# Retention followed by a Mish feed-forward layer: the decay of later chunks' keys goes into k, and v is loaded as bf16

## The chip, the core and the metric

The kernel runs on one core of one Trainium2 chip. The metric is device time in microseconds (us) of one execution. The core has a matrix engine (PE; its weight loads are listed apart as PEld), a vector engine (DVE), a scalar engine (ACT), GpSimd (POOL), a sync engine (SP), and 16 DMA engines that all queues share. In this kernel POOL issues nearly all loads, SP issues stores and DMA transposes.

## The reference

Eight batches, eight heads, 576 positions, 64 values per head. Retention is attention without a softmax: scores are multiplied by a power of a per-head decay. Its output goes through a two-layer feed-forward block (512 to 2048 to 512) with Mish between.

```python
def _attn_ref(q, k, v):
    scale = 1.0 / np.sqrt(D_)
    scores = scale * np.matmul(q, k.transpose(0, 1, 3, 2))
    gamma = 1.0 - 2.0 ** (-5.0 - np.arange(H))
    rel = pos[:, None] - pos[None, :]
    Dmat = np.where(rel >= 0, gamma[:, None, None] ** rel[None], 0.0)
    return np.matmul(scores * Dmat, v)
...
def _moe_ref(x, w_in, w_out):
    h = x @ w_in
    g = h * np.tanh(log1p(exp(h)))
    return g @ w_out
```

The decay from key position j to query position i is gamma to the power i - j, so it splits into a factor on q (gamma to the i, with 1/8 folded in) and a factor gamma to the minus j, which may stand on k or on v.

## The kernel before, in words

The 4608 rows are cut into 36 chunks of 128 rows. Chunks 0 to 7 are the first 128 positions of each batch; chunks 8 to 35 (`N0` = 8 and on) are the later ones, where a chunk may hold the last 64 positions of two batches. Four chunks form one of nine tiles `t`. The schedule is written out by hand: what stands first in the program is issued first on each engine.

The first eight chunks have their own path (`f_transpose`, `f_scores`, `f_out`), which applies the decay as a full matrix `dmask` and takes v unscaled; `f_state` scales a copy of their v with `gv` (L257) for the running state.

The later chunks go through these steps:

- `load(n)` or `load_part(n, part)` issues the transfers of q, k and v from POOL's queue (L325, and L329 for the chunks of two half batches). q and k land in `qkraw`, v in `vraw`, all as f32. For chunks 10 to 17 `load` first copies one element of an earlier v (L313), so that POOL waits until that v has landed. Later loads are paced by `tick` (L1045), a one-element copy of a result of the running tile, for which POOL waits.
- `step_p(n)`, "P", multiplies q and k with `gqk` on DVE and writes bf16 into `qks` (L341, two instructions per chunk). The column for k is all ones.
- `step_v(n)`, "V", multiplies v with `gv` and writes bf16 into `vs` (L348): on DVE for chunks 8 to 15, on POOL for chunks 16 to 35.
- `step_t(n)` transposes `qks` into `qkT`: on PE with a copy by ACT for chunks below 16, and by a DMA transpose from SP (L370) for the others.
- `states(n)` makes products of k in `qks` and `vs` (L428), which DVE adds into running states (L452, L450); `step_s` makes the scores (L382), `step_m` masks them (L388); `outputs` multiplies masked scores with `vs` (L484) and `outputs_end` adds the part of the earlier state (L500). `visit`, or `visit_first` and `visit_second`, run these for two chunks at a time, once in about 14 us.

Beside them PE works through the feed-forward layer: `g1` (L570, L575) with Mish on ACT (L586), and the second product from seven half-size products per tile (`seven`, L662), whose sums of operands DVE makes (L653, and L643 for the weights) and whose results DVE, ACT and POOL add up. In the last tile the first product is also made from seven products (`last`, L778). Their sums go through `both` and `z` (L790 to L808), for which `vraw` buffers are used, and `one`, in a `vs` buffer.

Of the kernel before, what the change touches and what calls it, by code (L numbers as in the profile page):

```python
# [9 lines left out]
F32 = mybir.dt.float32  # L10
BF16 = mybir.dt.bfloat16
AX = mybir.ActivationFunctionType
OP = mybir.AluOpType
# [3 lines left out]
def kernel(  # L17
# [21 lines left out]
    P = 128  # L39
# [4 lines left out]
    KC = d_model // P  # L44
    NCH = 4
    NPE = 16
    NV = 16
    PF = 5


# [102 lines left out]
    nc.vector.tensor_scalar(ident, dist, 0.0, None, op0=OP.is_equal)  # L153

    gqk = consts.tile([P, 5, 2, H], F32)
    nc.vector.memset(gqk, 1.0)
    gq = gqk[:, :, 0, :]
    gv = consts.tile([P, 5, H], F32)
    warm = consts.tile([P, 1], F32)

    def keep_warm(n, pool=ps_o, name="ops"):
# [146 lines left out]
    def load(n):  # L308
        if n >= n_chunks:
            return  # L310
        if N0 + 2 <= n < NPE + 2:

            nc.gpsimd.tensor_copy(landed[:, n % 2:n % 2 + 1], live[n - 2]["v"][:, H - 1, D - 1:D])  # L313
        for part in range(3):
            load_part(n, part)

    def load_part(n, part):
        b, c = chunks[n]
        if n not in live:
            qkr = io.tile([P, 2, H, D], F32, name="qkraw")  # L320
            live[n] = {"qkr": qkr, "v": io.tile([P, H, D], F32, name="vraw", bufs=7)}
        qkr, vr = live[n]["qkr"], live[n]["v"]
        for t, src in (((qkr[:, 0], q), (qkr[:, 1], k), (vr, v))[part],):
            if c < 4:
                nc.gpsimd.dma_start(  # L325
                    out=t, in_=src[b, :, ds(P * c, P), :].rearrange("h p d -> p h d"))
            else:
                for e in range(2):
                    nc.gpsimd.dma_start(  # L329
                        out=t[ds(64 * e, 64)],  # L330
                        in_=src[b + e, :, ds(512, 64), :].rearrange("h p d -> p h d"))

    def step_p(n):
        c = chunks[n][1]
        qks = io.tile([P, 2, H, D], BF16, name="qks", bufs=4)
        live[n]["qks"] = qks
        slots = qks.rearrange("p i (g x y) d -> p (i g) y x d", x=2, y=2)
        heads = live[n]["qkr"].rearrange("p i (g y x) d -> p (i g) y x d", x=2, y=2)
        factors = gqk[:, c].rearrange("p i (g y x) -> p (i g) y x", x=2, y=2)
        for y in range(2):  # L340
            nc.vector.tensor_tensor(slots[:, :, y], heads[:, :, y],  # L341
                                    factors[:, :, y].unsqueeze(3).to_broadcast([P, NP, 2, D]), op=OP.mult)

    def step_v(n):
        c = chunks[n][1]
        vs = tok.tile([P, H, D], BF16, name="vs")
        engine = nc.vector if n < NV else nc.gpsimd
        engine.tensor_tensor(vs, live[n]["v"], gv[:, c, :].unsqueeze(2).to_broadcast([P, H, D]), op=OP.mult)  # L348
        live[n]["vs"] = vs

    def step_t(n):
        flat = live[n]["qks"].rearrange("p i h d -> p (i h d)")
# [416 lines left out]
    def last(t):  # L769

        gts[t] = gp.tile([P, nF, NCH * P], BF16, name="gT")
        flat = gts[t].rearrange("p f i -> p (f i)")
        tt = nc.vector.tensor_tensor
        crossed = []

        def small(to, i, b, start=False):
            for c in range(hK):
                nc.tensor.matmul(to, lhsT=w7[i][:, c, b, :], rhs=x7[i][:, c, :], start=(start and c == 0),  # L778
                                 stop=(c == hK - 1), skip_group_check=True)

        def pair(b, between, adds=0):

            across = ps_h.tile([P, 2, hT], F32, name="hp")
            along = ps_sc.tile([P, 2, hT], F32, name="sc")
            small(across[:, 0], 3, b, True)
            small(across[:, 1], 4, b)
            small(along[:, 1], 6, b, True)
            small(along[:, 0], 1, b)
            both = io.tile([P, H, D], F32, name="vraw", bufs=7).rearrange("p h d -> p (h d)")
            act(both, across.rearrange("p a i -> p (a i)"))  # L790
            one = tok.tile([P, H, D], BF16, name="vs").rearrange("p h d -> p (h d)").bitcast(F32)
            act(one, along[:, 0])
            run(crossed)
            z = io.tile([P, H, D], F32, name="vraw", bufs=7).rearrange("p h d -> p (h d)")
            z = z.rearrange("p (a i) -> p a i", a=2)
            nc.gpsimd.tensor_tensor(z[:, 0], both[:, 0:hT], both[:, hT:2 * hT], op=OP.add)  # L796
            nc.gpsimd.tensor_tensor(z[:, 1], z[:, 0], one, op=OP.add)
            for _ in range(adds):
                behind_visit.pop(0)()
            between()  # L800
            small(across[:, 0], 5, b)
            small(across[:, 1], 2, b)
            small(along[:, 0], 7, b)
            o = 2 * b * NCH * P
            tt(z, z, across, op=OP.subtract)
            tt(z, along, z, op=OP.add)
            to = flat[:, ds(o, 6 * hT)].rearrange("p (a i) -> p a i", a=2)[:, :, 0:hT]
            crossed.append(lambda: nc.scalar.activation(to, z, AX.Mish))  # L808
            crossed.append(lambda: nc.scalar.activation(flat[:, ds(o + hT, 2 * hT)],
                                                        across.rearrange("p a i -> p (a i)"), AX.Mish))  # L810

        sums_at = {0: 1, 2: 6, 3: 5, 4: 7}
        g_sum(t - 1, 2)
        for b in range(nB - 1):
            pair(b, lambda: unit(t - 1, 2 * b), {3: 2, 4: 1}.get(b, 0))
            if b in sums_at:
                g_sum(t - 1, sums_at[b])
            unit(t - 1, 2 * b + 1)
        pair(nB - 1, lambda: unit(t - 1, 12), 1)
        unit(t - 1, 13)  # L820
        run(crossed)
        g1(t, nF - 2)
        g1(t, nF - 1, (ps_st, "st"))
# [61 lines left out]
    def att(n, steps):  # L885
        if n >= n_chunks:
            return
        for step in steps:
            {"P": step_p, "V": step_v, "T": step_t}[step](n)

    nc.scalar.activation(dmask, dmask, AX.Exp, bias=lnd[:, 0:1])
    for h in range(H):
# [84 lines left out]


    ps = {0: 0, 4: 1, 8: 2, 11: 3}
    vs = {0: 0, 5: 1, 9: 2, 13: 3, 18: 4, 19: 5}  # L980
    ts_ = {4: 0, 7: 1, 12: 2, 14: 3, 19: 4, 21: 5}
    FIRST = {1: (0, 0), 2: (1, 0), 3: ("turn", 1), 5: (0, 1), 6: (1, 1)}
    for u in range(24):
        j, w = divmod(u, 4)
        halved[0] = 2 if u < 1 else 0
        if u in FIRST:
            what, of = FIRST[u]
            if what == "turn":
                f_k0_copy(of, f_k0(of), (dve, act))
            else:  # L990
                first_states(of, what)
                if what:
                    first_states_copy(of, act)
        if u in ps:
            att(N0 + ps[u], "P")
        if u == 11:
            step_m(N0)
        if u in vs:
            att(N0 + vs[u], "V")
        if u in (1, 2):  # L1000
            f_state(1, u + 1, nc.vector)
        for what in {7: "W4", 9: "W6 W3 W1", 19: "S1", 21: "S6"}.get(u, "").split():
            w_sum(int(what[1])) if what[0] == "W" else g_sum(1, int(what[1]))
        if w == 0 and j > 0:
            if j < 5:
                load(N0 + j + 3)
            else:
                more_loads(N0 + j + PF)
        if u == 10:
            units = states(N0)  # L1010
            units[0]()
            step_s(N0)
            units[1]()
            run(sums)
        elif u == 16:
            att(N0 + 4, "P")
            visit(N0, ((ps_o, "ops"), (ps_h, "hp")), (act, act), masked=False)
            g_sum(1, 2)
            run(sums)
            att(N0 + 5, "P")  # L1020
            step_m(N0 + 2)
        elif u == 22:
            visit(N0 + 2, ((ps_h, "hp"), (ps_h, "hp")), (act, act))
        if u in (13, 20):
            run(casts, dve if u == 13 else act)
        if u in ts_:
            att(N0 + ts_[u], "T")
        if u < nF:
            g1(1, u)
            flush()  # L1030
        else:
            unit(1, u - nF)
# [9 lines left out]
    def tick(t, i):  # L1042

        f = done.get(t, 0)
        nc.gpsimd.tensor_copy(held[:, i % 2:i % 2 + 1], gts[t][:, f, 0:1])  # L1045

    W_IN = {3: 1, 4: 2, 8: 6, 10: 5, 11: 7}
    for t in range(NS, nT - 1):
        for i in range(nF):
# [39 lines left out]
                rest()  # L1089
            if w == 0 and n + 2 == NPE:  # L1090
                tick(t, i)
            if w in ((4,) if n + 2 < NPE else (0, 1)) and n <= NPE - 2:
                for m in (0, 1) if w == 4 else (w,):
                    att(n + 2 + m, "V")
            if n + 2 >= NPE and w == (6 if n + 2 == NPE else 3) and n + 4 < n_chunks:
                tick(t, i)
                att(n + 4, "V")
                att(n + 5, "V")
            if w == 7 and n + 4 == NPE:
                att(n + 5, "T")  # L1100
            if w == (4 if n <= NPE - 2 else 7) and n + 4 >= NPE:
# [67 lines left out]
```

## Time and profile before

| what | value |
|---|---|
| time, median of 3 runs | 290.36 us (288.36 to 295.45) |
| the profiled execution | 288.53 us, with a span of 286.8 us |
| busy: PE, DVE, ACT, POOL | 276.7, 215.5, 162.1, 172.0 us |
| granted PE clock | 1.00 throughout |
| transfers from POOL (q0) | 14256 packets, 30.15 MB |
| transfers from SP (q1) | 26656 packets, 14.69 MB |
| v loads | 24 of 256 KB, 8 of 128 KB; median 5.4 and 5.3 us to landing |

The span is the time from the first to the last instruction that the profiler recorded; the execution's own time holds 1.7 us more around it. Busy times are sums over instructions of an engine. Bytes are counted as they land, so a transfer that casts f32 to bf16 counts half of what it reads.

### The profile page before, as it was taken

What the parts mean: (1) busy time and instruction counts of PE and PEld (TensorE: products, weight loads), DVE (VectorE), ACT (ScalarE), POOL (GpSimd) and SP (SyncE); (2) the same over time, 40 slices, a digit from 0 to 9 for tenths busy, and PEclk for the clock granted to TensorE, in tenths of its full rate; (3) what the DMA queues carried; (4) which work ended last, traced back from release to release, by engine and by line L of the source; (5) the groups of instructions that cost most, each with busy time, mean ns of one, the idle gap of its engine ahead of it and who ended that gap; (6) DMA issues with size and microseconds to landing.
All of it is one profiled execution on the core that took longest, in us unless ns stands there. A gap on an engine that the chain in (4) does not pass through costs nothing.

```text
span 286.8 us, 8923 instructions
## 1 busy us (share of the span) xinstructions
PE 276.7 (96%) x3818; PEld 192.9 (67%) x3854; DVE 215.5 (75%) x302; ACT 162.1 (57%) x286; POOL 172.0 (60%) x243
## 2 busy tenths in 40 slices
PE   7799999999999999999999999999999999999994
PEld 3466775556876667666766666667666766888783
DVE  4740459999999996896599757974899194777783
ACT  5566415777776564565465555564566556476620
POOL 8686861687793999697929682969240000469500
PEclk9999999999999999999999999999999999999999
DMA  7999999978799994979599999697968001200323
GB/s 150 205 204 205 204 238 220 305 186 210 190 215 197 166 279 122 210 189 233 145 153 209 141 209 204 167 206 189 154 101 146 2 3 73 75 1 3 108 92 94
DMA packets 41545, 45.94 MB, mean 160 GB/s; under 512 B 23841, under 2 KB 31265, under 8 KB 41505
## 3 DMA queue, kind: packets, MB, share of 16 engines
q0 software_dynamic: 14256, 30.15, 50.1%
q1 hardware_dynamic: 26656, 14.69, 26.4%
q8 instruction: 30, 0.49, 0.8%
q10 hardware_dynamic: 592, 0.52, 0.6%
q14 instruction: 11, 0.08, 0.1%
HBM read 36.70 MB, written 9.44 MB: 161 GB/s over the span
## 4 chain that ended last, share of the span: by engine, by line
PE 69%; DMA 15%; DVE 7%; POOL 5%; issue 2%; ACT 1%; POOLq 0%; ACTq 0%; DVEq 0%
PE hp L570 28%; PE ops L662 27%; DMA w_out_t<-in_moe_w_out_dram 4%; DMA vraw<-in_v_dram 4%; DMA w_in_t<-in_moe_w_in_dram 4%; PE st L662 2%; DMA qkraw<-in_k_dram 2%; PE hp L662 2%; PE hp L778 2%; DVE qks L341 2%; PE sc L778 1%; PE sc L428 1%; PE sc L382 1%; PE sc L849 1%; POOL gT L107 1%
## 5 line engine op out<-in xcount | busy, mean ns | idle before, releaser
L570 PE MATMUL hp<-xT,w_in_t 128*128 128x512 bf16 x439 | 111.8, 379 | 1.8 <-issue 0.3
L586 ACT ACTIVATE gT<-hp 128x512 bf16<-128x512 f32 x129 | 76.9, 600 | 46.6 <-PE hp L570 42.2
L570 PEld LDWEIGHTS <-w_in_t 128*128 128x128 bf16 x474 | 45.3, 98 | 41.0 <-issue 0.9
L662 PEld LDWEIGHTS <-room 128*128 128x128 bf16 x608 | 58.8, 98 | 13.9 <-DVE room L653 0.3
L341 DVE TENSOR_TENSOR qks<-qkraw,gqk 128x512 bf16<-128x512 f32 x56 | 48.1, 908 | 10.1 <-issue 5.1
L653 DVE TENSOR_TENSOR room<-gT 128x2048 bf16<-128x2048 bf16 x40 | 50.8, 1289 | 1.1 <-ACT gT L586 1.1
L1045 POOL COPY held<-gT 128x1 bf16<-128x1 bf16 x58 | 23.0, 397 | 32.9 <-ACT gT L586 32.9
L662 PE MATMUL ops<-room,room 128*128 128x256 bf16 x320 | 40.1, 273 | 0.3 <-DVE room L653 0.2
L796 POOL TENSOR_TENSOR vraw<-vraw 128x256 f32<-128x256 f32 x7 | 6.5, 924 | 37.9 <-ACT vraw L790 37.8
L662 PEld LDWEIGHTS <-gT 128*128 128x128 bf16 x256 | 24.5, 98 | 6.2 <-ACT gT L586 0.4
L388 DVE TENSOR_TENSOR sm<-sc,mask 128x1024 bf16<-128x1024 f32 x14 | 17.1, 1218 | 11.7 <-PE sc L382 11.1
L348 POOL TENSOR_TENSOR vs<-vraw,gv 128x512 bf16<-128x512 f32 x20 | 25.5, 1297 | 0.0
L662 PE MATMUL ops<-w_out_t,room 128*128 128x256 bf16 x208 | 25.3, 273 | 0.0
L325 POOL DMA_DIRECT2D vraw<-in_v_dram x24 | 21.3, 886 | 2.5 <-DMA w_out_t<-in_moe_w_out_dram 1.4
L325 POOL DMA_DIRECT2D qkraw<-in_q_dram x24 | 21.7, 904 | 1.5 <-issue 1.2
L325 POOL DMA_DIRECT2D qkraw<-in_k_dram x24 | 21.2, 884 | 0.0
L452 DVE TENSOR_TENSOR total<-sc,total 128x256 f32<-128x256 f32 x32 | 13.5, 422 | 2.2 <-PE sc L428 1.4
L512 ACT CAST xT<-hp 128x512 bf16<-128x512 f32 x19 | 10.3, 589 | 7.6 <-PE hp L500 7.6
L662 PE MATMUL ops<-room,gT 128*128 128x256 bf16 x112 | 13.7, 272 | 0.2 <-ACT gT L586 0.2
L575 PE MATMUL hp<-xT,w_in_t 128*128 128x256 bf16 x92 | 13.8, 273 | 0.0
L575 PEld LDWEIGHTS <-w_in_t 128*128 128x128 bf16 x92 | 9.0, 98 | 5.4
L175 DVE COPY room<-gT 128x1024 bf16<-128x1024 bf16 x4 | 3.2, 828 | 9.7 <-DMA gT<-in_q_dram 9.7
(186 smaller groups left out, 423.6 us busy)
## 6 DMA issues: line engine op xcount, KB each, us to landing
out_dram<-res SPq DMA_DIRECT2D x29, 256.0 KB, 4.8
qkraw<-in_q_dram POOLq DMA_DIRECT2D x24, 256.0 KB, 6.1
qkraw<-in_k_dram POOLq DMA_DIRECT2D x24, 256.0 KB, 6.4
vraw<-in_v_dram POOLq DMA_DIRECT2D x24, 256.0 KB, 5.4
w_out_t<-in_moe_w_out_dram POOLq DMA_DIRECT2D x4, 512.0 KB, 11.3
w_in_t<-in_moe_w_in_dram POOLq DMA_DIRECT2D x3, 512.0 KB, 10.1
out_dram<-res SPq DMA_DIRECT2D x9, 128.0 KB, 2.4
gT<-in_k_dram POOLq DMA_DIRECT2D x8, 128.0 KB, 6.9
```

Source lines behind the costliest of these rows:

```text
L325: nc.gpsimd.dma_start(out=t, in_=src[b, :, ds(P * c, P), :].rearrange("h p d -> p h d"))
L341: nc.vector.tensor_tensor(slots[:, :, y], heads[:, :, y], factors[:, :, y].unsqueeze(3).to_broadcast([P, NP, 2, D]), op=OP.mult)
L348: engine.tensor_tensor(vs, live[n]["v"], gv[:, c, :].unsqueeze(2).to_broadcast([P, H, D]), op=OP.mult)
L388: nc.vector.tensor_tensor(sm.rearrange("p e x n i -> p (e x n) i"), live[n]["sc"].rearrange("p e x n i -> p (e x n) i"), mask.unsqueeze(1) ...
L452: nc.vector.tensor_tensor(new[:, k], st[:, j, x], total[b], op=OP.add)
L512: copy(xts[t][:, :, ds(P * s, 2 * P)].rearrange("p h (x j i) -> p j h x i", x=2, j=2)[:, j], both[j])
L570: nc.tensor.matmul(to, lhsT=w, rhs=x, start=first, stop=last)
L575: nc.tensor.matmul(to[:, ts(j, n)], lhsT=w, rhs=x[:, ts(j, n)], start=False, stop=False, skip_group_check=True)
L586: nc.scalar.activation(gts[t][:, f, :], hp, AX.Mish)
L653: engine.tensor_tensor(to, g_half(t, *a), g_half(t, *b), op=op_)
L662: nc.tensor.matmul(bank[:, half, :], lhsT=g[:, f, ts(half, P)], rhs=w[:, f, :], start=(f == 0 and half == 0 and not add), stop=(f == hF - ...
L1045: nc.gpsimd.tensor_copy(held[:, i % 2:i % 2 + 1], gts[t][:, f, 0:1])
```

## The change

The factor gamma to the minus j moves from v to k for the later chunks. The k column of `gqk`, ones before, becomes `gv`, so the multiplication that `step_p` already does brings it in. `step_v` disappears with its calls, on DVE and on POOL, as do the ticks directly ahead of those of its calls that ran on POOL (not the ticks ahead of loads). v is loaded straight into `vs` in bf16: source f32, destination bf16, a casting transfer at the same place in POOL's queue. `vs` has 13 buffers where it had 6, `qks` 6 where it had 4, and the 7 f32 buffers of `vraw` are gone; `both` and `z` of the last tile use `qks` buffers. The first eight chunks keep their scaled copy of v.

```diff
     gqk = consts.tile([P, 5, 2, H], F32)
-    nc.vector.memset(gqk, 1.0)
     gq = gqk[:, :, 0, :]
-    gv = consts.tile([P, 5, H], F32)
+    gv = gqk[:, :, 1, :]
...
-            nc.gpsimd.tensor_copy(landed[:, n % 2:n % 2 + 1], live[n - 2]["v"][:, H - 1, D - 1:D])
+            nc.gpsimd.tensor_copy(landed[:, n % 2:n % 2 + 1], live[n - 2]["vs"][:, H - 1, D - 1:D])
...
-            live[n] = {"qkr": qkr, "v": io.tile([P, H, D], F32, name="vraw", bufs=7)}
-        qkr, vr = live[n]["qkr"], live[n]["v"]
+            live[n] = {"qkr": qkr, "vs": tok.tile([P, H, D], BF16, name="vs", bufs=13)}
+        qkr, vr = live[n]["qkr"], live[n]["vs"]
...
-        qks = io.tile([P, 2, H, D], BF16, name="qks", bufs=4)
+        qks = io.tile([P, 2, H, D], BF16, name="qks", bufs=6)
...
-    def step_v(n):
-        c = chunks[n][1]
-        vs = tok.tile([P, H, D], BF16, name="vs")
-        engine = nc.vector if n < NV else nc.gpsimd
-        engine.tensor_tensor(vs, live[n]["v"], gv[:, c, :].unsqueeze(2).to_broadcast([P, H, D]), op=OP.mult)
-        live[n]["vs"] = vs
...
-            both = io.tile([P, H, D], F32, name="vraw", bufs=7).rearrange("p h d -> p (h d)")
+            both = io.tile([P, 2, H, D], BF16, name="qks", bufs=6).rearrange("p i h d -> p (i h d)").bitcast(F32)
...
-            z = io.tile([P, H, D], F32, name="vraw", bufs=7).rearrange("p h d -> p (h d)")
+            z = io.tile([P, 2, H, D], BF16, name="qks", bufs=6).rearrange("p i h d -> p (i h d)").bitcast(F32)
...
-        if u in vs:
-            att(N0 + vs[u], "V")
...
-            if w in ((4,) if n + 2 < NPE else (0, 1)) and n <= NPE - 2:
-                for m in (0, 1) if w == 4 else (w,):
-                    att(n + 2 + m, "V")
-            if n + 2 >= NPE and w == (6 if n + 2 == NPE else 3) and n + 4 < n_chunks:
-                tick(t, i)
-                att(n + 4, "V")
-                att(n + 5, "V")
```

More of the change, by code (lines that the diff above doesn't have):

```diff
@@ L46 @@
     NPE = 16
-    NV = 16
     PF = 5
@@ L788, in pair @@
             small(along[:, 0], 1, b)
-            both = io.tile([P, H, D], F32, name="vraw", bufs=7).rearrange("p h d -> p (h d)")
+            both = io.tile([P, 2, H, D], BF16, name="qks", bufs=6).rearrange("p i h d -> p (i h d)").bitcast(F32)
             act(both, across.rearrange("p a i -> p (a i)"))
-            one = tok.tile([P, H, D], BF16, name="vs").rearrange("p h d -> p (h d)").bitcast(F32)
+            one = tok.tile([P, H, D], BF16, name="vs", bufs=13).rearrange("p h d -> p (h d)").bitcast(F32)
             act(one, along[:, 0])
             run(crossed)
-            z = io.tile([P, H, D], F32, name="vraw", bufs=7).rearrange("p h d -> p (h d)")
+            z = io.tile([P, 2, H, D], BF16, name="qks", bufs=6).rearrange("p i h d -> p (i h d)").bitcast(F32)
             z = z.rearrange("p (a i) -> p a i", a=2)
@@ L888, in att @@
         for step in steps:
-            {"P": step_p, "V": step_v, "T": step_t}[step](n)
+            {"P": step_p, "T": step_t}[step](n)
     nc.scalar.activation(dmask, dmask, AX.Exp, bias=lnd[:, 0:1])
@@ L979 @@
     ps = {0: 0, 4: 1, 8: 2, 11: 3}
-    vs = {0: 0, 5: 1, 9: 2, 13: 3, 18: 4, 19: 5}
     ts_ = {4: 0, 7: 1, 12: 2, 14: 3, 19: 4, 21: 5}
```

## The prediction

> **What bounds the kernel now.** I read the page's busy row first, then busy time by stage, then who waited for whom on PE, and last single stretches of the PE timeline.
>
> ```profile
> span 286.8 us, 8923 instructions
> PE 276.7 (96%) x3818; PEld 192.9 (67%) x3854; DVE 215.5 (75%) x302; ACT 162.1 (57%) x286; POOL 172.0 (60%) x243
> ```
>
> PE is busy for 276.7 of 286.8 us, so 10.1 us at most can be won without taking matmuls away, and the change takes none away. The view by stages (length, then busy us of PE, PEld, DVE, ACT and POOL, the granted clock, the DMA share, GB/s) says where those 10.1 us lie:
>
> ```profile
> 0.00:20.00 20.00, 16.27 (x186) 9.34 (x189) 11.75 (x39) 11.43 (x21) 15.49 (x29) 1.00 1.02 185
> 20.00:264.00 244.00, 241.74 (x3476) 168.13 (x3508) 188.12 (x243) 143.38 (x253) 151.58 (x211) 1.00 0.81 164
> 264.00:286.80 22.80, 18.65 (x161) 15.42 (x159) 15.67 (x21) 7.29 (x14) 4.97 (x5) 1.00 0.31 93
> ```
>
> The start has 3.73 us of idle PE and the end 4.15 us. In the 244 us between, where every operation of this change lies except a memset and the sums of the last tile, PE idles for 2.26 us. A busy PE can still be a slow one, so I compared spacings (start, length, engine and line, operation, tiles, count):
>
> ```profile
> 71.17 1.04 PE L662 MATMUL st<-w_out_t,gT 128*128 128x256 bf16 x8
> 72.04 0.61 PE L362 MATMUL hp<-ident,qks 128*128 128x128 bf16 x8
> ...
> 277.48 1.91 PE L662 MATMUL ops<-room,room 128*128 128x256 bf16 x16
> 279.22 1.91 PE L662 MATMUL hp<-room,room 128*128 128x256 bf16 x16
> ```
>
> At 71 us, in the stretch where DVE is 99% busy, 8 matmuls take 72.04 - 71.17 = 0.87 us, 109 ns each. In the tail, with all operands ready, 16 take 279.22 - 277.48 = 1.74 us, 109 ns each. So PE runs at its own pace already. Its waits say the same (total us, times, longest); these are among the largest after the first 12 us:
>
> ```profile
> PE sc L212 <- DVE room L216: 0.4, 2, 0.3
> PE ops L662 <- DVE room L653: 0.2, 1, 0.2
> PE ops L662 <- ACT gT L586: 0.2, 1, 0.2
> ```
>
> The Trainium skill (Perfetto Trace Analysis, "Identifying the Most-Contended Engine") warns of this reading: matmul busy time flatters PE, and weight-load busy time is the better measure. By its 67% a third of the span would be open; the equal spacing of 109 ns does not agree, and I follow the spacing. What would follow if PE had room is the third rival.
>
> The chain of waits none the less runs through DMA and DVE until 77 us, and there lies what the change touches (start, length, what):
>
> ```profile
> 36.91 12.21 DMA vraw<-in_v_dram
> ...
> 50.61 6.68 DMA qkraw<-in_k_dram
> 57.39 1.29 DVE qks L341 x2
> ...
> 74.81 1.20 DVE vs L348 x2
> 76.00 1.15 DVE room L653
> 77.20 1.92 PE ops L662 x16
> ```
>
> This chain had no slack at 77.20, but PE waited only 0.23 us there (the 0.2 in the view of waits): it had other work until then.
>
> **The change, part by part.**
>
> ```profile
> L341 DVE TENSOR_TENSOR qks<-qkraw,gqk 128x512 bf16<-128x512 f32 x56 | 48.1, 908 | 10.1 <-issue 5.1 <-DMA qkraw<-in_q_dram 2.6 <-DMA qkraw<-in_k_dram 2.5
> L348 POOL TENSOR_TENSOR vs<-vraw,gv 128x512 bf16<-128x512 f32 x20 | 25.5, 1297 | 0.0
> L348 DVE TENSOR_TENSOR vs<-vraw,gv 128x512 bf16<-128x512 f32 x8 | 5.3, 684 | 0.0
> ```
>
> *Scaling of v, removed.* DVE loses 8 instructions, 5.3 us, between 51.2 and 85.9 us. Four of them lie on the chain behind 57.39 (0.60 + 0.60 + 1.20 = 2.4 us), so L653 can end 2.4 us sooner. PE gets of that its wait, 0.23 us; the rest is early data for a busy engine. POOL loses 20 instructions, 25.5 us, and 9 of its 58 one-element copies at L1045 (397 ns each, 3.6 us). L341's median is 685 ns and its mean 908, and its long ones (2.13 us for two, at 92.4) coincide with L348 on POOL (2.95 us from 92.5); without it, DVE regains up to 48.1 - 56 x 0.685 = 9.7 us. After 86 us none of this is on PE's path: 0 us. The cover is PE's queue of ready matmuls. If it were gone, DVE's 5.3 + 9.7 us would count.
>
> *Decay in k.* step_p multiplies the same tile with another factor column: same instruction, 0 us. The memset at L156 (0.12 us on DVE at 4.61) goes; DVE waits 0.61 us for PE at 7.07 behind it, so 0 us. The exponential that made gv now writes into gqk, 40 values either way.
>
> *v by casting transfers.* Each issue stays on POOL's queue at its old place: 24 of 882 ns and 8 of 691 ns. Nearest rows for a casting issue: the two 256-column w_in loads and three of 512 columns average 769 ns (L86), w_out 836 ns (L89), with 4 runs per partition against 8 for v; I take no change, and up to 0.2 us more each would still leave POOL 25.5 + 3.6 - 32 x 0.2 = 22.7 us lighter.
>
> What the transfer itself costs is not in the trace; nothing there writes v's 64 values as 128 bytes. Rows (the last three values are clock, DMA share and GB/s, counted as landed):
>
> ```profile
> 24.00:28.00 4.00, 3.95 (x29) 2.79 (x29) 0.00 (x0) 2.89 (x5) 2.13 (x4) 1.00 1.24 206
> 46.00:48.00 2.00, 2.00 (x37) 1.33 (x37) 2.00 (x3) 1.52 (x3) 0.00 (x0) 1.00 1.05 219
> 92.00:96.00 4.00, 4.00 (x24) 2.19 (x23) 4.00 (x6) 2.81 (x6) 4.00 (x5) 1.00 1.26 134
> ```
>
> At 46 us plain loads of q, k and v drain in 256-byte runs at 219 GB/s: 262 KB take 1.20 us. At 24 us casting loads with long runs land 206 GB/s: v's 131 KB would take 0.64 us. At 92 us, with transposes in flight, 134 GB/s is nearly the worst rate at a full share: 0.98 us. If a run costs what it costs now, whatever its length, it stays 1.20 us. So -0.56 to 0 us a transfer by the rows; I take 0, because v keeps its 1024 runs. The worse case, above every row, is the second rival.
>
> *Waits and buffers.* PE's state products (L428) and output products (L484) now wait for the transfer of v itself instead of L348. Queued behind such a wait would be all of PE. For chunk 10 the transfer has landed by 58.64 us (POOL's copy L313 that waits for it starts then) and the product starts at 68.16: 9.5 us of cover. A load now overwrites what PE reads, with 13 buffers: the first reuse, chunk 21 at 97.15 us, needs chunk 8's products, done by 69.3. Sums of the last tile move from vraw's buffers into the 6 of qks, reused three pairs later; the last transposes out of them are issued at 215-217 us and land in 10.6 us at most, before L790 at 245.9. All 0 us. SP's queue is unchanged.
>
> **Sum.** -0.23 us (L653's wait), with the issue gaps beside it -0.3. Span 286.8 - 0.3 = 286.5; the profiled execution has 288.53 - 286.8 = 1.73 around it: 288.2. The median of the runs shown is 290.36, 1.83 above the profiled execution, so 290.0.
>
> **The rivals.**
> 1. *All of PE's small gaps close.* Lighter DVE and POOL take away the whole 2.26 us between 20 and 264: 290.36 - 2.26 = 288.1. For: several gaps stand behind DVE or ACT. Against: most are single gaps of 0.05 us named "issue". Chance 0.12.
> 2. *The casting transfers are slow, and k comes late.* Between 40 and 58 us the DMA share is 1.01 to 1.06, so extra transfer time delays what is queued behind it. Two v transfers (chunks 8 and 9) are ahead of k of chunk 10, which ends the wait at 57.30. The chain behind has 2.4 us of removed DVE work as cover and 0.23 us of wait already. At twice 1.20 us the delay is 2.4 and just covered; from there it decides. At three times it is 4.8 - 2.4 = 2.4 us of stall: 290.36 + 2.4 = 292.8; at four times 295.2; a 2% loss takes more than that, with later loads late too. Against: no row is over 1.20 us. Chance 0.13. The Trainium skill (DMA: Bandwidth & Descriptors, "Specifications") speaks for it: under 512 bytes a transfer turns into read-modify-write, and v's runs go from 256 to 128. The trace shows plain 256-byte runs at 219 GB/s landed where long casting runs read twice 206, which agrees that short runs are slow, but cannot tell 128 from 256.
> 3. *PE has room, and DVE is the bound where it is full.* From 57 to 100 us DVE is 99% busy. It would give back its 5.3 us of L348 and, at 92 to 96 us, 1.1 us of lengthened L341: 290.36 - 6.4 = 284.0. Against: the spacing at 71 us. Chance 0.05.
>
> That the change does not do what it says I exclude: no L348 is left on any queue, and every other engine's order stands.
>
> **How the numbers follow.** The forecast has 0.70. Range: rival 1 less 1.1 us for runs that stand apart (the two lower ones differ by 2.0) gives 287.0; rival 2 at three times with 0.7 on top gives 293.5. About 2% (5.8 us) is what a measurement of this kernel can tell from no change. Faster by more: rival 3, 0.05. Slower by more: half of rival 2, since waits on later loads could add up, 0.07. Within: 0.88.
>
> **What would show it.** Right: PE busy again near 276.7 with no wait over 0.3 us after 20 us, DVE near 215.5 - 15 = 200, POOL near 143, L341's mean near 685 ns, the step at 77.20 no longer behind DVE. Wrong: PE waits on in_v_dram or on qks at 57 to 80 us, or v's time to landing well above 5.4 us.

## The result, and the profile after

The changed kernel takes 287.56 us in the median (287.32 to 287.91, 7 runs), the kernel before 288.92 us on the same chip (288.36 to 295.45, 7 runs). The ratio is 0.9941, with a 95% interval of 0.9914 to 0.9967: 0.6% faster, below the 2% that count as a difference here, but clear of 1. Ratios leave disturbed executions out; the medians hold them. The profiled executions agree: 288.53 us before, 287.56 after, with spans of 286.8 and 285.9.

The page after, its busy row, the queue of POOL's transfers, and the groups that the change touches (lines are shifted: L341 is now L339, L1045 is L1033, L653 is L644, L662 is L653):

```profile
span 285.9 us, 8908 instructions
PE 276.9 (97%) x3818; PEld 192.7 (67%) x3854; DVE 197.3 (69%) x293; ACT 162.1 (57%) x286; POOL 144.2 (50%) x214
...
q0 software_dynamic: 41136, 26.48, 56.1%
...
L339 DVE TENSOR_TENSOR qks<-qkraw,gqk 128x512 bf16<-128x512 f32 x56 | 35.4, 685 | 4.5 <-issue 2.9
...
vs<-in_v_dram POOLq DMA_DIRECT2D x24, 128.0 KB, 5.1
```

PE is as busy as before (276.9 against 276.7 us). DVE lost 18.2 us and POOL 27.8 us, and a span that is 0.9 us shorter is all that is left of these 46 us. The multiplication of q and k, which had a mean of 908 ns, now has its median of 685 ns as its mean. The transfers carry fewer bytes (26.48 against 30.15 MB) in nearly three times the packets (41136 against 14256) and their packet times add up to a larger share of the engines' span (56.1 against 50.1%).

By stages (length, then busy us of PE, PEld, DVE, ACT and POOL, clock, DMA share, GB/s):

```profile
0.00:20.00 20.00, 17.38 (x189) 9.70 (x192) 11.92 (x38) 11.71 (x21) 16.13 (x30) 1.00 1.01 192
20.00:264.00 244.00, 242.17 (x3484) 168.74 (x3516) 171.03 (x236) 143.83 (x254) 124.31 (x182) 1.00 0.86 149
264.00:285.90 21.90, 17.35 (x148) 14.23 (x147) 14.37 (x20) 6.52 (x12) 3.75 (x4) 1.00 0.31 97
```

In the first 20 us PE's busy time leaves 2.62 us where it left 3.73, in the long middle stage 1.83 where it left 2.26. Most of the latter is not idling. Both pages count 3818 matmuls and 3854 weight loads, so 36 matmul records are missing. In two later runs, `e_plain` and `e_memset`, the page counts 3854 of each. In both, PE is busy for the whole of the middle stage; this is the first:

```profile
20.00:264.00 244.00, 244.00 (x3517) 168.68 (x3516) 170.84 (x236) 143.62 (x254) 123.28 (x182) 1.00 0.71 164
```

With 33 more matmuls recorded than after (3517 against 3484), nothing is left of the 1.83 us. So the prediction's 2.26 us were some 0.4 us of pauses, and what went is the 0.43 us between the two figures. In the timeline before, PE has two marked pauses in this stage; after, none:

```profile
77.20 1.92 PE L662 MATMUL ops<-room,room 128*128 128x256 bf16 x16 [0.23 <-DVE room L653]
...
171.72 0.59 PE L570 MATMUL hp<-xT,w_in_t 128*128 128x512 bf16 x2 [0.26 <-issue]
```

The step that the prediction built on, in the timeline of DVE, before and then after:

```profile
75.92 2.35 DVE L653 TENSOR_TENSOR room<-gT 128x2048 bf16<-128x2048 bf16 x2
```

```profile
72.40 1.22 DVE L379 TENSOR_TENSOR sm<-sc,mask 128x1024 bf16<-128x1024 f32 x1
73.53 2.35 DVE L644 TENSOR_TENSOR room<-gT 128x2048 bf16<-128x2048 bf16 x2
```

The sums (L653 before) start at 73.53 instead of 75.92 us, 2.4 us earlier, and the 16 matmuls of PE that read them follow their neighbours without a pause. The chain of waits, which ran through DMA and DVE here, now runs through PE alone (start, length, what), and PE's waits after the first 20 us hold nothing of DVE:

```profile
76.14 0.16 PE sc L419 x16
76.30 0.13 PE hp L491 x16
76.43 1.85 PE ops L653 x16
78.29 0.21 PE hp L561
```
```profile
PE ops L162 <- DVE room L125: 1.3, 1, 1.3
PE st L191 <- DMA gT<-in_q_dram: 0.4, 1, 0.4
PE st L240 <- DVE room L224: 0.4, 1, 0.4
...
PE ops L653 <- ACT gT L577: 0.2, 1, 0.2
```

(The first three lie before 20 us.) The pause at 171.72, for which the timeline names no releaser, is gone too. The matmul milestones add up as follows. The first matmul of `g1` starts 0.54 us earlier (16.35 instead of 16.89), the scores at 87 us 0.83 earlier, those at 184 us 1.21, the last group of matmuls 1.30 (279.67 instead of 280.97). So the gain was not the one step of 0.3 us: 0.54 us came before 17 us, where no v of a later chunk was scaled yet, 0.29 us between 17 and 87 us, and 0.47 us after that.

### The profile page after: what moved, and what is told of

It is laid out like the page before. It is cut to its first block, busy times and chain, and to the rows that moved or that the text cites. A ratio compares the mean times of both kernels' runs of the same rounds, so it can differ in the third digit from the quotient of the medians.

```text
span 285.9 us, 8908 instructions
## 1 busy us (share of the span) xinstructions
PE 276.9 (97%) x3818; PEld 192.7 (67%) x3854; DVE 197.3 (69%) x293; ACT 162.1 (57%) x286; POOL 144.2 (50%) x214
## 3 DMA queue, kind: packets, MB, share of 16 engines
q0 software_dynamic: 41136, 26.48, 56.1%
## 4 chain that ended last, share of the span: by engine, by line
PE 91%; DVE 2%; DMA 2%; issue 2%; POOL 1%; ACT 1%; POOLq 0%; ACTq 0%; DVEq 0%
PE hp L561 36%; PE ops L653 27%; PE hp L566 5%; PE st L653 3%; PE hp L653 2%; PE hp L769 2%; PE sc L419 2%; DMA gT<-in_q_dram 2%; PE sc L373 2%; PE sc L769 1%; PE sc L840 1%; POOL gT L106 1%; PE sc L353 1%; PE hp L491 1%; DVE room L214 1%
## 5 line engine op out<-in xcount | busy, mean ns | idle before, releaser
L653 PEld LDWEIGHTS <-room 128*128 128x128 bf16 x608 | 58.8, 98 | 13.6
L644 DVE TENSOR_TENSOR room<-gT 128x2048 bf16<-128x2048 bf16 x40 | 49.1, 1246 | 1.4 <-ACT gT L577 1.4
L1033 POOL COPY held<-gT 128x1 bf16<-128x1 bf16 x49 | 17.9, 366 | 49.5 <-ACT gT L577 49.5
L653 PE MATMUL ops<-room,room 128*128 128x256 bf16 x320 | 40.1, 273 | 0.1
L339 DVE TENSOR_TENSOR qks<-qkraw,gqk 128x512 bf16<-128x512 f32 x56 | 35.4, 685 | 4.5 <-issue 2.9
L787 POOL TENSOR_TENSOR qks<-qks 128x256 f32<-128x256 f32 x7 | 6.5, 926 | 49.4 <-ACT qks L781 49.3
L653 PEld LDWEIGHTS <-gT 128*128 128x128 bf16 x256 | 24.5, 98 | 6.2 <-ACT gT L577 0.4
L653 PE MATMUL ops<-w_out_t,room 128*128 128x256 bf16 x208 | 25.3, 273 | 0.0
L323 POOL DMA_DIRECT2D vs<-in_v_dram x24 | 21.6, 901 | 2.4 <-DMA w_out_t<-in_moe_w_out_dram 1.2
L653 PE MATMUL ops<-room,gT 128*128 128x256 bf16 x112 | 13.7, 273 | 0.2 <-ACT gT L577 0.2
L653 PE MATMUL ops<-w_out_t,gT 128*128 128x256 bf16 x80 | 10.4, 273 | 0.0
L450 ACT CAST ssb<-total 128x768 bf16<-128x768 f32 (+3 forms) x13 | 10.1, 779 | 0.0
```

The source lines that it names most:

```text
L323: nc.gpsimd.dma_start(out=t, in_=src[b, :, ds(P * c, P), :].rearrange("h p d -> p h d"))
L339: nc.vector.tensor_tensor(slots[:, :, y], heads[:, :, y], factors[:, :, y].unsqueeze(3).to_broadcast([P, NP, 2, D]), op=OP.mult)
L450: copy(lows[:, 0:k], new[:, 0:k])
L644: engine.tensor_tensor(to, g_half(t, *a), g_half(t, *b), op=op_)
L653: nc.tensor.matmul(bank[:, half, :], lhsT=g[:, f, ts(half, P)], rhs=w[:, f, :], start=(f == 0 and half == 0 and not add), stop=(f == hF - ...
```

## The experiments

All times are medians, all ratios are against the kernel before on the same chip. Two numbers serve as a ruler in the traces: the time from the first to the last group of score matmuls of the later chunks, in which PE does the same work in each of these kernels (165.82 us after, 166.59 before), and the start of `g1`.

### Both kernels again

> The kernel before, once more, to see how far two profiles of one program differ. If PE's early progress depends on chance (arrival of the first q and k), the first matmul of g1 moves by some tenths from its 16.89 us and the ratio to the kernel before is 1.000 within 0.003. If the 0.54 us by which the changed kernel reached g1 earlier belongs to the change, this profile has 16.8 to 17.0 again.

> The changed kernel, once more. Theory A (PE is the bound; the gain is the 0.23 us wait at 77 us plus gaps of 0.05 to 0.3 us behind busy POOL and DVE): ratio 0.995 to 0.998, PE progress from g1's first matmul to the last matmul shorter by 0.6 to 0.9 us than in the kernel before, whatever the start does. Theory B (the gain is the start): that stretch is the same in both within 0.2 us, and the ratio stays at 0.994.

Measured: 288.76 us, ratio 0.999 (0.9967 to 1.0012), and 287.44 us, ratio 0.9957 (0.9942 to 0.9972). The change gains 0.4 to 0.6%. The changed kernel repeats its ruler to the hundredth, 165.82 us; the kernel before took 167.47 this time, with other pauses than in its first profile:

```profile
46.97 0.64 PE L242 MATMUL sc<-room,room 128*64 128x128 bf16 x16 [0.42 <-ACT room L226]
...
98.93 0.25 PE L484 MATMUL hp<-sm,vs 64*64 64x64 bf16 x7 [0.64 <-issue]
```

So in the kernel before PE is at the edge of waiting in several places, and in the changed one it is not.

### Half of the scaling back

In each, v of the chunks named lands as f32 again and is multiplied, now by ones, where it was before; the decay stays in k. `vraw` has 4 buffers in these two and `vs` 9.

```diff
+    ones = consts.tile([P, 5, H], F32)
+    nc.vector.memset(ones, 1.0)
+    SCALED = lambda n: n >= NPE     # e_dve_scaled: n < NPE
...
+        engine.tensor_tensor(vs, live[n]["v"], ones[:, c, :].unsqueeze(2).to_broadcast([P, H, D]), op=OP.mult)
```

> The changed kernel with POOL's part undone: v of chunks 16 to 35 lands in f32 and POOL multiplies it (by ones, the decay stays in k), with the ticks ahead of it; chunks 8 to 15 come by casting transfers and lose DVE's scaling. Theory A: the wait of PE behind DVE at 77 us is gone (0.23 us) but the small gaps after 86 us are back: ratio to the kernel before about 0.998 to 1.000, slower than the changed kernel by 0.3 to 0.6 us; L339's mean back at about 850 to 900 ns. If all the gain is DVE's: as fast as the changed kernel.

> The changed kernel with DVE's part undone: v of chunks 8 to 15 lands in f32 and DVE multiplies it (by ones); chunks 16 to 35 come by casting transfers, nothing on POOL. Theory A: PE waits 0.2 to 0.3 us for DVE near 77 us again, later gaps stay closed: ratio 0.996 to 0.999, 0.2 to 0.4 us slower than the changed kernel; L339's mean near 685 ns. If all the gain is POOL's: as fast as the changed kernel.

Measured: with POOL's part back 288.89 us, ratio 0.9995 (0.9975 to 1.0015); with DVE's part back 289.06, ratio 1.0011 (0.9984 to 1.0037). Each half, put back alone, takes the whole gain away. Two halves that each cost the whole cannot be two shares of one sum, which pointed to something that both kernels had in common beside the scaling. The rulers read 166.34 and 165.97 us, 0.52 and 0.15 over after, while the last group of scores starts 1.47 and 1.39 us later than after. So most of the loss lies ahead of the ruler, in the first 62 us.

### The start

Since 0.54 us had come before `g1`, the memset that the change removed was put back, and in the kernel before it was moved to a place where DVE waits anyway.

```diff
# e_memset (after)
     gqk = consts.tile([P, 5, 2, H], F32)
+    nc.vector.memset(gqk, 1.0)
# b_memset_early (before): the two lines moved up, behind the memset of lnd
     nc.vector.memset(lnd, -0.5 * math.log(D))
+    gqk = consts.tile([P, 5, 2, H], F32)
+    nc.vector.memset(gqk, 1.0)
```

> The changed kernel with the memset of gqk (0.12 us on DVE at 4.6 us) put back, nothing else. In the six profiles so far g1's first matmul starts at 16.0 and 16.4 us without a memset there and at 16.5 to 17.2 us with one. Theory B (part of the gain is the start, by way of that memset): first matmul at 16.5 to 17.2 us again, 0.3 to 0.7 us (0.1 to 0.25%) slower than the changed kernel, so ratio near 0.998. Theory A (the start is chance, the gain is gaps further on): as fast as the changed kernel, ratio 0.994 to 0.997, and the stretch from g1's first matmul to the last matmul is 263.3 us as in the changed kernel.

> The kernel before with that memset moved ahead, into DVE's wait at 1.2 us; the scaling of v stays on DVE and POOL. Theory B: 0.1 to 0.25% faster than the kernel before, ratio 0.9975 to 0.999. Theory A: ratio 1.000, and PE's progress after g1's first matmul is longer than 263.3 us by 0.8 to 2.4 us, as in the two profiles of the kernel before.

Measured: 287.51 us, ratio 0.9955 (0.9938 to 0.9971), and 288.79, ratio 0.9998 (0.9969 to 1.0026). The memset has nothing to do with it.

### The transfer: plain, and twice

```diff
# e_plain: v lands as f32, PE reads the upper half of each value as bf16
+            live[n] = {"qkr": qkr, "vraw": tok.tile([P, H, D], F32, name="vs", bufs=8)}
+            live[n]["vs"] = live[n]["vraw"]....bitcast(BF16)....[:, :, :, 1]
# e_twice: each v is loaded once more into a tile that nobody reads
+        if part == 2:
+            todo.append((tok.tile([P, H, D], BF16, name="spare", bufs=4), v))
```

> The changed kernel without the cast: v lands in f32 by plain transfers, and PE reads the upper half of each value in place as bf16 (cut off instead of rounded), two bytes out of every four. Nothing scales or casts v on any engine, so only the transfer differs (and the stride of PE's reads, and 8 buffers for 13). If the cast costs DMA time that is hidden (Theory A): DMA share of 20 to 264 us back at about 0.8, packets of POOL's queue back near 14000, time as the changed kernel within 0.3%. If the many small packets are what keeps PE free of gaps: gaps of 0.2 to 0.6 us come back and the ratio goes to 0.998 or more. If PE reads strided bf16 more slowly, L420 and L476 take longer in the profile and the ratio rises by that.

> The changed kernel with every casting transfer of v issued twice, the second into a tile that nothing reads: twice the DMA time for v and 32 more issues on POOL (about 28 us, what POOL had gained). Measured so far: POOL's queue took 267 us more engine time with the cast, 0.6 us of all 16 engines more per chunk than a plain 1.2 us. So v costs 3.6 us here where it cost 1.2 before: the second rival of the prediction at three times. Rival: k of chunk 10 lands 3.6 us later than in the changed kernel, PE waits 1 to 3 us between 57 and 80 us, ratio 1.000 to 1.006. Theory A with more slack than reckoned: PE hardly waits, ratio 0.995 to 0.999.

Measured: plain 287.69 us, ratio 0.9953 (0.993 to 0.9977); twice 291.93 us, ratio 1.0054 (1.0016 to 1.0091). The queue's line in the two pages, plain and then twice:

```profile
q0 software_dynamic: 14256, 30.15, 44.6%
```
```profile
q0 software_dynamic: 70320, 30.16, 76.4%
```

The cast is not needed for the gain. What it costs the engines needs care, because the share adds up the times of packets. The shares, times the span, give this queue 127 us with plain loads (44.6% of 285.4), 160 us with v cast (56.1% of 285.9) and 220 us with v cast twice (76.4% of 287.5): 2.1 us of packet time on all 16 engines for each of the 28 second loads. But casting packets overlap. This is the queue in the kernel with two casts, from 57 to 58 us:

```profile
DMA packets 948, 0.19 MB, mean 186 GB/s; under 512 B 931, under 2 KB 931, under 8 KB 948
```
```profile
q0 software_dynamic: 948, 0.19, 203.5%
```

An engine has two packets under way at once here. Nearly all of the 931 small ones carry one cast run each, and v of a chunk has 1024 runs. So an estimate for one casting transfer is 1.1 us, or 0.9 us if the 17 large packets beside them are taken off at 161 ns (worked out below). That is inside the prediction's rows, 0.64 to 1.20 us, and little more than the 0.78 us of a plain load on its boundary. It is hidden. Two of them, with 32 more issues on POOL, are not, though the place is another one than the second rival's: PE waits for transposes that are late at 98 us, not for k of chunk 10 at 57. The profiled execution took 289.24 us and the median is 291.93, so these two waits are only a part of the loss.

```profile
98.38 0.32 PE L376 MATMUL sc<-qkT 64*64 64x64 bf16 x16 [0.25 <-DMA qkT<-qks]
...
99.73 0.26 PE L494 MATMUL hp<-qkT,last 64*64 64x64 bf16 x8 [0.90 <-SPq L407]
```

### Work put back where nobody waits for it, ticks, and the algebra alone

```diff
# e_dve_idle, e_pool_idle (after): multiplications of the old size and place, n < NPE on DVE or n >= NPE on POOL
+        scrap = tok.tile([P, H, D], BF16, name="scrap", bufs=2)
+        fixed = dmask.rearrange("p h x -> p (h x)")[:, 0:H * D].rearrange("p (h d) -> p h d", h=H)
+        engine.tensor_tensor(scrap, fixed, gv[:, c, :].unsqueeze(2).to_broadcast([P, H, D]), op=OP.mult)
# e_ticks (after): the nine ticks alone
+                tick(t, i)
# b_decay_in_k (before): decay in k, v multiplied by ones
-    gv = consts.tile([P, 5, H], F32)
+    gv = gqk[:, :, 1, :]
+    ones = consts.tile([P, 5, H], F32)
```

> The changed kernel with 8 DVE multiplications of the old size (128x512, f32 times factor into bf16) put back where V stood for chunks 8 to 15, but out of a constant tile into one that nobody reads: DVE's work without anyone waiting for its result. Theory A (PE's gaps come from DVE's and POOL's time, since sums and copies that PE needs end later): L653's end before 77 us is again about 2.4 us later and PE's wait of about 0.2 us there is back; PE's stretch from the first to the last scores is longer than 165.82 us by 0.2 to 0.6; time +0.1 to +0.6 against the changed kernel (287.5). Rival D (what counted was PE's wait for the scaled v itself): no gap, 165.82 us, 287.5.

> The changed kernel with 20 POOL multiplications of the old size put back where V stood for chunks 16 to 35, out of a constant tile into one that nobody reads, without the ticks ahead of them. Theory A: POOL busy near 144 + 25 = 169 us, L339's mean back from 685 to about 900 ns (its time is lengthened by POOL's multiplication, whatever that reads), one or two PE gaps of 0.2 to 0.6 us between 86 and 220 us, first to last scores 166.0 to 166.5 us, time +0.2 to +0.8. Rival D: L339 may lengthen, but PE keeps 165.82 us and the time 287.5.

> The changed kernel with the 9 removed one-element copies (ticks) put back alone: POOL waits for a result of the running tile before the loads that follow. Theory A: nothing but POOL's queue is later, L339's mean stays near 685 ns, PE keeps 165.82 us, 287.5 within 0.4. Rival E (the ticks hold back loads, and these are what PE's gaps come from): gaps with issue or DMA named between 86 and 220 us, and 288 to 288.8.

> The kernel before with the decay moved into k and v multiplied by ones in the same places, with the same buffers, plain loads and ticks as before: the algebra alone, without what it saves. It has one memset of 40 values fewer on a larger tile and one of 40 more. Theory A: same as before, ratio 1.000 (288.8), L341's mean near 908 ns, PE's first to last scores 166.4 to 167.5 us. Rival F (the numbers in k or the buffers matter, as by fewer active bits in the operands or another order): 287.5, nearer to the changed kernel.

Measured: DVE's work 287.57 us, ratio 0.9945 (0.9918 to 0.9972); ticks 287.16, ratio 0.9927 (0.9899 to 0.9954); the algebra alone 289.46, ratio 1.0002 (0.9969 to 1.0036). So neither DVE's 5.3 us of multiplications nor the ticks cost anything that these runs can tell, theory A of `e_dve_idle` fails, and the algebra alone gains nothing.

POOL's work gave 291.88 us, ratio 1.0076 (1.004 to 1.0111), but this experiment is spoilt by its edit: `dmask` is no constant. ACT writes results into it later (L688), and had to wait for POOL's reading. PE's waits, and ACT's timeline:

```profile
PE ops L662 <- ACT dmask L688: 2.7, 1, 2.7
```
```profile
111.59 0.59 ACT L688 COPY dmask<-ops 128x512 f32<-128x512 f32 x1 [4.91 <-POOL scrap L349]
```

Still, two things can be read from its trace. Its ruler is 169.02 us; the stretch with that wait is 2.87 us longer than after, and the other 0.33 us of the difference lie in small delays, most of them after 186 us. The profiled execution, 290.32 us, is 1.6 us below the median, so the trace need not show all of the loss. And the multiplication of q and k is slow again; with DVE's work back instead it is not (POOL's kernel first, then DVE's):

```profile
L339 DVE TENSOR_TENSOR qks<-qkraw,gqk 128x512 bf16<-128x512 f32 x56 | 48.9, 922 | 4.9 <-issue 2.0
```
```profile
L339 DVE TENSOR_TENSOR qks<-qkraw,gqk 128x512 bf16<-128x512 f32 x56 | 35.4, 685 | 1.7 <-issue 1.5
```

### What the kernels have in common

Sorted by ratio, the kernels fall into two groups, which scaling work does not explain. What separates them is how fast q and k land. From 40 to 46 us POOL's queue moves all the data but 0.01 MB: the last loads of v of the first chunks (L118) and those of q, k and v of the first later chunks, all f32 in runs of 256 bytes, and all issued before any v of a later chunk was scaled. That queue, in the kernel before and in the one with plain loads of v (packets, MB, share of 16 engines in these 6 us; packets of an engine overlap, so it can pass 100%):

```profile
q0 software_dynamic: 390, 1.34, 103.3%
```
```profile
q0 software_dynamic: 578, 1.93, 96.9%
```

The transfers have the same source, shape and packets of some 3.4 KB. A packet takes 1.033 x 16 x 6 us / 390 = 254 ns in the one and 0.969 x 16 x 6 / 578 = 161 ns in the other. What differs is where they land. `gv` was a tile of 5 x 8 x 4 = 160 bytes ahead of every tile that a load lands in. The change makes it a part of `gqk`, and everything behind it moves down by 160 bytes. In the compiled programs the first `qkraw` buffer lies at byte 96160 of each partition before, which is 160 past a multiple of 256, and at 96000 after, which is 375 x 256; the sizes of the large tiles are multiples of 256, so `gT`, `vs` and the others share this. A run of 64 f32 values is 256 bytes: after, each fills one block of 256, before, each lies across two. My tile `ones` has 160 bytes as well, so three experiments that were meant to take the change apart had the old places.

The same loads in the windows of 40 to 42 us, before, with DVE's part scaled, after, and with DVE's work put back idle (the last two values are the share of the engines and the GB/s that landed):

```profile
40.00:42.00 2.00, 2.00 (x24) 1.51 (x23) 1.11 (x1) 0.68 (x1) 0.88 (x1) 1.00 1.02 234
```
```profile
40.00:42.00 2.00, 2.00 (x25) 1.55 (x23) 1.22 (x1) 0.79 (x1) 0.19 (x1) 1.00 1.05 242
```
```profile
40.00:42.00 2.00, 2.00 (x22) 1.41 (x20) 1.22 (x1) 1.01 (x1) 0.88 (x1) 1.00 1.05 345
```
```profile
40.00:42.00 2.00, 1.95 (x24) 1.59 (x23) 0.12 (x1) 0.00 (x0) 0.88 (x1) 1.00 1.05 350
```

The engines are about equally full, and nearly a half more lands. All the kernels:

| kernel | bytes past 256 | scaling work in it | GB/s, 40 to 42 us | q, k to landing (us) | `g1` starts (us) | ratio |
|---|---|---|---|---|---|---|
| before | 160 | all | 234 | 6.1, 6.4 | 16.89 | 1 |
| before again | 160 | all | 234 | 5.9, 6.4 | 16.48 | 0.999 |
| b_memset_early | 160 | all | 244 | 5.9, 6.6 | 16.99 | 0.9998 |
| e_pool_scaled | 160 | POOL's | 242 | 6.0, 6.2 | 17.22 | 0.9995 |
| e_dve_scaled | 160 | DVE's | 242 | 5.5, 6.4 | 16.78 | 1.0011 |
| after | 0 | none | 345 | 4.4, 5.0 | 16.35 | 0.9941 |
| after again | 0 | none | 339 | 4.6, 5.2 | 16.02 | 0.9957 |
| e_memset | 0 | none | 335 | 4.4, 5.2 | 16.33 | 0.9955 |
| e_plain | 0 | none | 338 | 4.6, 5.4 | 16.16 | 0.9953 |
| e_ticks | 0 | ticks | 334 | 4.6, 5.4 | 16.20 | 0.9927 |
| e_dve_idle | 0 | DVE's | 350 | 4.4, 4.9 | 17.88 | 0.9945 |

(b_decay_in_k, at 160 bytes, had 239 GB/s and a ratio of 1.0002. Its profiled execution took 295.76 us. e_dve_idle was granted a PE clock of 0.91 in its first 20 us, and its `g1` is late; its ruler of 165.83 us is that of after.)

Left out are e_twice and e_pool_idle, whose added traffic and spoilt wait decide their time; both are at 0 bytes and had 334 and 354 GB/s. The groups do not overlap in rate, whatever else was in the kernel, and the kernels of the table not in time to landing or in ratio (q and k take 6.8 and 7.6 us to landing in e_twice, behind its added loads). With DVE's work in both and POOL's in neither, 160 bytes give 1.0011 (e_dve_scaled) and 0 bytes 0.9945 (e_dve_idle). What else differs in this pair is that in the first v of chunks 8 to 15 comes by plain loads and PE needs the product. Plain loads cost nothing in e_plain, and in the trace of e_dve_scaled PE waits for no `vs`: after 20 us its waits are 0.62 us for ACT's cast of v of the first chunks, named below, and 0.18 us near 271 us, which every kernel has. The Trainium skill (DMA: Bandwidth & Descriptors, "How a descriptor splits into AXI transactions") has a rule that fits: a descriptor that does not start on a multiple of 256 bytes starts its first transaction at the boundary below, in beats of 32 bytes. An estimate by that rule: a run of 256 bytes that starts at 160 needs 8 + 5 = 13 beats instead of 8, 1.63 times as many. The packets here take 254 / 161 = 1.58 times as long, so the trace agrees; but the page tells it of reading, and here the written side is the one off its boundary.

How the loads reach the clock can be seen at 43 to 47 us, where ACT casts v of the first chunks as it lands. ACT's timeline with DVE's part scaled, 160 bytes, and then after:

```profile
44.22 1.14 ACT L226 CAST room<-room 128x512 bf16<-128x512 f32 x2 [2.00 <-DMA room<-in_v_dram]
46.62 0.62 ACT L226 CAST room<-room 128x512 bf16<-128x512 f32 x1 [1.25 <-DMA room<-in_v_dram]
```
```profile
42.06 1.14 ACT L224 CAST room<-room 128x512 bf16<-128x512 f32 x2 [0.26 <-DMA room<-in_v_dram]
43.58 0.62 ACT L224 CAST room<-room 128x512 bf16<-128x512 f32 x1 [0.38 <-DMA room<-in_v_dram]
```

The last of them is 3.0 us earlier. In the slow-landing group PE waits for it in some profiles (0.42 us before again, 0.62 with DVE's part scaled, nothing in the first profile of before), in the other group in none. With all matmul records there, the middle stage shows PE idle for 0.55 us in b_memset_early, at 160 bytes, and for none in e_plain and e_memset, at 0.

What stays open: a kernel that differs from after, or from before, by 160 bytes of padding alone was not run, so the time that the places are worth is read from kernels that differ in more. POOL's part at 0 bytes was only run in the spoilt experiment. The 0.33 us of that trace are the best number for it; by e_dve_scaled, which lacks it at 160 bytes, taking it out gives 1.0011 (0.9984 to 1.0037), which leaves room for a gain of 0.16% (0.5 us) at most.

## Why the prediction was right, and what it missed

**The bound.** Right. PE stays at 276.9 us, matmuls keep the spacing of 109 ns, and 46 us less work on DVE and POOL are worth some tenths of a microsecond: DVE's work costs nothing that the ratios show (0.9945 with it, 0.9941 to 0.9957 without), POOL's some 0.33 us by the trace. That this is close to the forecast's 0.3 us is luck, since the forecast had it all from DVE. One reading was wrong without harm: the 2.26 us of idle PE between 20 and 264 us were for the most part missing records. The spacing in the timeline of PE after, 0.87 us for 8 matmuls (71.50 less 70.63):

```profile
70.63 1.04 PE L653 MATMUL st<-w_out_t,gT 128*128 128x256 bf16 x8
71.50 0.61 PE L353 MATMUL hp<-ident,qks 128*128 128x128 bf16 x8
```

The third rival, that DVE is the bound where it is full, is out.

**Scaling of v, removed.** The sizes came out: DVE 197.3 us where near 200 was expected, POOL 144.2 where 143 was, the mean of the q and k multiplication exactly 685 ns. That POOL's multiplication was what lengthened it is now shown: 880 to 931 ns in the kernels with it, 682 to 686 in those without, DVE's own scaling or not. The Trainium skill (SBUF — State Buffer, "Who interferes with whom") says that DVE and GpSimd share one pair of ports under an exclusive lock, and that a DVE instruction with two inputs in SBUF contends with a GpSimd instruction that reads SBUF; the trace agrees. The wait of 0.23 us at 77 us went as forecast, with L653 2.4 us earlier as forecast, but not only by the removed multiplications. In e_dve_idle, with the four multiplications in DVE's queue again, the sums start 0.86 us ahead of the scores of their visit, 2.13 after and 0.27 before, and PE does not wait. There k of chunk 10 was no longer what DVE waited for, as it had before for 0.21 us at 57.39. Nor is there a pause in e_pool_scaled, at 160 bytes without DVE's scaling, so by these two traces either of the two is enough. "After 86 us none of this is on PE's path: 0 us" was off by the 0.33 us of POOL's part.

**Decay in k.** This is the step that failed. The prediction says of the exponential that made gv: "now writes into gqk, 40 values either way", and costs it at nothing. As work it is nothing. But the tile of 160 bytes that it no longer needs stood ahead of every load's target, and without it a packet of plain loads of 256-byte runs takes 161 ns instead of 254. The missed term is most of the gain, though no run isolates it. In the first pair of profiles it is the 0.54 us before `g1`, where every profile at 160 bytes starts at 16.48 or later and every one at 0 bytes and full clock at 16.38 or earlier, and the part of the pauses between 20 and 100 us that hangs on loads. By the ratios of e_dve_scaled and e_dve_idle it is 0.66%, an estimate of 1.9 us, with 0.8 to 3.0 by their intervals.

**v by casting transfers.** Right in size, by another reckoning. "It stays 1.20 us" came from 219 GB/s, which was the rate of runs off their boundary; a plain v at 338 GB/s takes 262 KB / 338 = 0.78 us. The cast takes 0.9 to 1.1 us by the estimate above, where 0.64 to 1.20 was the range. Packet time, 2.1 us, would overstate it; what was written ahead of `e_twice` about three times the cost rests on packet time. "v keeps its 1024 runs" was true and left out a count: plain, 16 runs go in one packet, cast, each run is a packet of its own, 1024 against 64 for a chunk, which is the whole rise of 28 x 960 = 26880 packets. v's time to landing went from 5.4 to 5.1 us, with faster loads of q and k ahead of it.

**Waits, buffers, ticks.** Right. There is no wait of PE on v's transfer and none above 0.2 us after 20 us in that view, and the nine ticks are worth nothing.

**The rivals.** The first, that all small gaps close, is nearest in time, 288.1 against 287.56, and that is luck. Its 2.26 us were mostly missing records, the pauses that were there are worth some 0.4 us, and 0.54 us came before 20 us; it also stood on 290.36, 1.4 us too high. The second did not come: one cast stays below 1.20 us and nothing is lost (0.9953 without the cast). The 219 GB/s that it took as a sign that short runs are slow came from where they landed: on their boundary the same runs reach 338. With twice the casts the kernel is 1.0% slower than after (1.0054 against 0.9955 or so). By the estimate these are 1.8 to 2.2 us, at most 1.8 times 1.20, where the rival still saw cover; but POOL has 32 more issues there, and PE waits in another place.

**The time.** 290.0 against 287.56: 1.4 us of the difference is that the sum was hung on the median of three runs, 290.36, which is 288.92 with more runs. The other 1.0 us is gain that the forecast did not have: in PE's milestones, 0.54 us before 17 us and 0.47 after 87 us. As a ratio, 0.9990 was forecast and 0.9941 measured.

## What to carry to other kernels

Removing or adding a small tile moves every tile behind it: after any edit to the constants, look at where the targets of short DMA runs begin. Here runs of 256 bytes did well on a multiple of 256 and badly 160 bytes past one; no other place was tried. When two halves of a change, each undone alone, both cost the whole gain, look for what the two experiments share before adding up shares. An engine that is 97% busy at its own spacing gives some tenths of a microsecond for 46 us of work taken off its neighbours, and more can lie in the loads ahead of it. Before idle time is read off busy time, compare the counts of matmuls and weight loads: records can be missing. And packet times of a DMA queue are no engine time where the share passes 100%.

## What the hardware showed that was not expected

- A load of 256-byte runs takes 254 ns for a packet of about 3.4 KB when the target starts 160 bytes past a multiple of 256, and 161 ns when it starts on one; from 40 to 42 us that is 234 to 244 GB/s against 334 to 354.
- A casting load is not packed: one packet for each run, 41136 packets where plain loads need 14256. Its packets overlap (share 203.5%), so 2.1 us of packet time for 1024 runs are an estimated 0.9 to 1.1 us of the engines, where a plain load takes 0.78 us.
- PE reads v with a stride of two values (the upper halves of f32) at hardly any loss: with plain loads the ruler is 165.94 us against 165.82.
